# One written order for all steps of a DeltaNet and mixer kernel in place of a planner

## The chip, the cores and the metric

The kernel runs on one core of one Trainium2 chip. The core has five engines with a queue of instructions each: TensorE (PE, matrix products; PEld is its weight load), VectorE (DVE), ScalarE (ACT), GpSimd (POOL) and SyncE (SP, which here only issues transfers). Every engine works through its queue strictly in order and waits on semaphores for the others. The metric is the device time of one execution in microseconds (us), as the median of several runs.

## The reference

The inputs are q, k and v of shape (4, 8, 768, 48), beta of (4, 8, 768), U (768 x 32), V (32 x 768), w_ch1 (384 x 1536) and w_ch2 (1536 x 384); the first four are fp32, the weights 64-bit. The first half is a linear attention with the delta rule, token by token for each of the 32 heads:

```python
k_n = k / (norm(k, axis=-1) + 1e-6)
state = zeros((B, H, D, D))
for t in range(S):
    y[:, :, t] = q[:, :, t] @ state              # per head
    v_old = k_n[:, :, t] @ state
    state += beta[:, :, t] * outer(k_n[:, :, t], v[:, :, t] - v_old)
```

The heads are then put side by side (x has shape 4 x 768 x 384), and the second half mixes tokens through a low rank product and channels through an MLP:

```python
u = x + (x.T @ U @ V).T          # over the tokens of a batch
out = u + relu(u @ w_ch1) @ w_ch2
```

## The kernel before, in words

**Tiling.** The 768 tokens of a batch are cut into 12 chunks of 64 tokens, and 6 chunks make a unit; there are 8 units, two to a batch. Within a chunk the token loop is replaced by matrix products and the inverse of a triangular matrix; between chunks runs a recurrence over the state. The MLP works on three groups of 256 tokens a batch.

**A unit.** `load` (its transfers at L531) brings k, q, v and a second copy of k into one of two slots, in pieces of 72 KB through the queues of SP and POOL (the first k pieces through ACT's too). `grams` turns k and q on TensorE (L633), copies them out on ACT (L648) and multiplies (`products`, L661); ACT and DVE take the diagonal blocks (L671, L674) and DVE masks the products with q (L692). `load_beta` (L551 to L577) brings beta over the region of X, turns it on TensorE and spreads it. `norms` works out 1/|k|^2 times beta and scales v (L610). `blocks` inverts the 32-wide diagonal blocks by substitution on DVE (L737 lays them out, L746 and L752 are the 32 steps, L759 returns them) and joins them to the inverses of 64-wide blocks on TensorE (L802, L816, L842 to L863). The units of batch 0 join 16-wide blocks first (L802 and L816).

**The recurrence.** `recur(b)` has for each of the 12 chunks: the product of the state with the k (L1051) on TensorE, its subtraction on DVE that gives z (L1064; in later batches the chain at L1010 to L1043), the state update's product (L1079), its addition on DVE (L1089), and the outputs (L925, L939), which ACT copies into X (L909). When the last chunk of a unit is out, the slot is free and the loads of the unit after next may start.

**Weights.** `load_weights` brings 14 slices of U, V, w_ch1 and w_ch2 as 64-bit numbers of two 32-bit words each into staging regions (the second half of X, `wide`, and hs), issued by SP (L1166; the first by POOL). DVE makes one fp32 word of each pair (L1193, L1199, L1205), with a copy by ACT between that writes the upper 16 bits (L1174), and forms sums of weights at L1119. A slice may be fetched when the slice before it in the same region has been unpacked.

**The MLP.** `front` forms u (L1372 to L1418). `wide` is the first product with 6 channel steps per group. Each step exists in two forms: plain, six matmuls of 128x128 by 256 columns, three to each half (L1475), or parted in four 64x64 quadrants (L410, `crossed`) with a small ACT copy between (L419, `swap`), which avoids a change of TensorE's tiling when it stands next to other quadrant work. ACT applies the relu (L1440), DVE forms sums (L1502, L1509) for a product scheme with 7 products in place of 8, and `narrow` is the second product (L1590) with DVE collecting (L1515) and SP storing (L1521, L1524).

**What sets the order.** Every function above is a generator that yields one step at a time: its engine, a cost, a form of TensorE, the PSUM bank that it takes and those that it gives back, or a list of keys that it needs first. `run` (L343 to L398) is a planner that works while the program is built. At each turn it works out when every waiting step could start (`start_of`, L315), with a clock per engine, costs that are written at the steps, a model of TensorE's clock (`pace`, L293: a factor of 1.9 for slow), of instruction fetches (`late`, L307) and of landings (`landing`, L125); among the steps that could start soonest it takes the one with the lowest place. The places are a table of some 250 entries (`PLACES`, L145), and entries ending in "quad" allow the parted form for a channel step (`form`, L332). All five queues come out of this one order.

```python
def op(engine, cost, mode=None, take=None, give=(), lat=None, ...)      # L103
begin(start(i), 22)                                                     # a part with its place
x = yield op("pe", 0.8, "F", take="pair", words=12, flow=0.64)          # a step of grams
yield need(("wide", i))                                                 # what must be written first
```

A key is emitted when the step that makes it has been written down; a list of needs so holds back the writing of a step. On the chip the program's semaphores hold what the data demand.

Of the kernel before, what the change touches and what calls it, by code (L numbers as in the profile page):

```python
# [1 line left out]

# [5 lines left out]

# [8 lines left out]

# [6 lines left out]

QUADS = ((0, 0), (1, 1), (1, 0), (0, 1))


@with_exitstack
def kernel(
    ctx: ExitStack,  # L30
    tc: tile.TileContext,
    q: bass.AP,
    k: bass.AP,
    v: bass.AP,
    beta: bass.AP,
    moe_U: bass.AP,
    moe_V: bass.AP,
    moe_w_ch1: bass.AP,
    moe_w_ch2: bass.AP,
    out: bass.AP,  # L40
):

    nc = tc.nc  # L50

# [16 lines left out]
    W2 = 2 + 2 * KT  # L68

    const = ctx.enter_context(tc.tile_pool(name="const", bufs=1))  # L70
    single = ctx.enter_context(tc.tile_pool(name="single", bufs=1))
    small = ctx.enter_context(tc.tile_pool(name="small", bufs=2))
    conv = ctx.enter_context(tc.tile_pool(name="conv", bufs=2))
    mix = ctx.enter_context(tc.tile_pool(name="mix", bufs=2))
    scratch = ctx.enter_context(
        tc.tile_pool(name="scratch", bufs=2, space=bass.MemoryType.DRAM)
    )
    psum = ctx.enter_context(
        tc.tile_pool(name="psum", bufs=1, space=bass.MemoryType.PSUM)
    )  # L80

    P = psum.tile([128, 8, 512], FP32, name="P")
    BANK = dict(pair=[0, 2, 4, 6], mix=[6, 7])

    clock = dict(port=0.0, pe=0.8, dve=0.8, act=0.8, pool=0.8, sp=0.8)
    state = dict(now=0.0, mode=None, hw=0.0, slow=1.9, lot=69, fetched=0.0, flow=0.0, span=0)
    free = dict(pair={x: 0.0 for x in range(4)}, mix={})
    done, parts, waits, ready, last = {}, {}, {}, {}, {}  # L90
    asked, missing, awaited, woken, quads = {}, {}, {}, [], set()
    LAT = dict(pe=0.22, dve=0.06, act=0.06, pool=0.1, sp=0.0)
    SWITCH, HOLD, STAY = 0.18, 0.18, 0.15
    LOT, FETCH = 256, 4.1
    SPAN, PHASE = 3.413, 2.0

    def dve(n):
        return (n + 151) / 1000.0

    def act(n):  # L100
        return 0.16 + n / 1200.0

    def op(  # L103
        engine, cost, mode=None, take=None, give=(), lat=None, rush=None, words=0, port=None, flow=None,
        after=(),
    ):
        return dict(
            after=after,
            flow=cost * 0.95 if flow is None else flow,
            e=engine, cost=cost, mode=mode, take=take, give=give, words=words + 0.4,  # L110
            port=engine == "pool" if port is None else port,
            rush=bool(give) if rush is None else rush, lat=LAT[engine] if lat is None else lat,
        )
# [4 lines left out]
    def emitted(key, after=0.0):  # L118
        done[key] = state["now"] + after
# [5 lines left out]
    def landing(packets, each=0.0205):  # L125
        state["hw"] = max(state["hw"], state["now"] + 1.0) + packets * each / 16
        return state["hw"] + 0.4 - state["now"]

    def advance(i, value, at):
        try:  # L130
            s, ready[i] = parts[i].send(value), at
        except StopIteration:
            waits.pop(i, None)
            return
        if isinstance(s, list):
            waits.pop(i, None)
            asked[i], missing[i] = s, {key for key in s if key not in done}
            for key in missing[i]:
                awaited.setdefault(key, []).append(i)
            if not missing[i]:  # L140
                woken.append(i)
        else:
            waits[i] = s

    PLACES = """  # L145
    add_up b0 i0 17.5; add_up b0 i1 115.48; add_up b0 i2 71; add_up b1 i1 10.76; add_up b1 i2 15.15
    add_up b2 i0 54.56; add_up b2 i1 63.94; add_up b2 i2 115.5; add_up b3 i0 -4.22; add_up b3 i1 62.29
    add_up b3 i2 42; blocks n1 40.91; blocks n2 26.26; blocks n3 92.86; blocks n4 49.5; blocks n5 78.95
    blocks n6 36.67; blocks n7 136.31; both -6; channels b0 i0 e1 24.46; channels b0 i0 e2 52.34
    channels b0 i0 e3 47.17; channels b0 i0 e4 51.28; channels b0 i0 e5 -8.66; channels b0 i1 e0 52.04  # L150
    channels b0 i1 e0 quad 1; channels b0 i1 e1 79.42; channels b0 i1 e2 120.05; channels b0 i1 e3 96.5
    channels b0 i1 e3 quad 1; channels b0 i1 e4 13.79; channels b0 i1 e5 26.76; channels b0 i2 e0 quad 1
    channels b0 i2 e1 88.32; channels b0 i2 e1 quad 1; channels b0 i2 e2 92.17; channels b0 i2 e2 quad 1
    channels b0 i2 e3 128.97; channels b0 i2 e4 12; channels b0 i2 e4 quad 1; channels b0 i2 e5 88
    channels b0 i2 e5 quad 1; channels b1 i0 e0 40.95; channels b1 i0 e0 quad 1; channels b1 i0 e1 59
    channels b1 i0 e1 quad 1; channels b1 i0 e2 96.8; channels b1 i0 e2 quad 1; channels b1 i0 e4 91
    channels b1 i0 e4 quad 1; channels b1 i0 e5 69.5; channels b1 i0 e5 quad 1; channels b1 i1 e1 123.7
    channels b1 i1 e1 quad 1; channels b1 i1 e2 47.06; channels b1 i1 e2 quad 1; channels b1 i1 e3 -2.83
    channels b1 i1 e4 -16.29; channels b1 i1 e4 quad 1; channels b1 i1 e5 99.12; channels b1 i1 e5 quad 1
    channels b1 i2 e0 62.73; channels b1 i2 e0 quad 1; channels b1 i2 e2 35.08; channels b1 i2 e3 93.63  # L160
    channels b1 i2 e3 quad 1; channels b1 i2 e4 -29.18; channels b1 i2 e5 10.16; channels b1 i2 e5 quad 1
    channels b2 i0 e0 107; channels b2 i0 e1 41.61; channels b2 i0 e2 12.5; channels b2 i0 e2 quad 1
    channels b2 i0 e3 100.05; channels b2 i0 e3 quad 1; channels b2 i0 e4 17.5; channels b2 i0 e5 68.5
    channels b2 i1 e0 -1.5; channels b2 i1 e0 quad 1; channels b2 i1 e1 107.29; channels b2 i1 e1 quad 1
    channels b2 i1 e2 -7.68; channels b2 i1 e2 quad 1; channels b2 i1 e3 -3.95; channels b2 i1 e4 33.5
    channels b2 i1 e4 quad 1; channels b2 i2 e0 0.4; channels b2 i2 e0 quad 1; channels b2 i2 e1 22.31
    channels b2 i2 e1 quad 1; channels b2 i2 e2 21.63; channels b2 i2 e2 quad 1; channels b2 i2 e3 7.38
    channels b2 i2 e3 quad 1; channels b2 i2 e4 90.57; channels b2 i2 e5 quad 1; copies 0; cut 9
    diagonals n0 h0 -0.5; diagonals n0 h1 107.22; diagonals n1 h0 48.5; diagonals n1 h1 -9.5; diagonals n2 h0 12
    diagonals n2 h1 67.42; diagonals n4 h0 15; diagonals n4 h1 22.77; diagonals n5 h0 66.26; diagonals n5 h1 66.6  # L170
    diagonals n6 h0 49.61; diagonals n6 h1 75; diagonals n7 h0 65.5; diagonals n7 h1 71.44; first 71.59
    first_of_last 8.76; front b0 i0 46.95; front b0 i0 quad 1; front b0 i1 41.01; front b0 i2 58.06
    front b1 i0 30.2; front b1 i1 45.12; front b1 i2 142.26; front b1 i2 quad 1; front b2 i0 46.76
    front b2 i0 quad 1; front b2 i1 6.48; front b2 i1 quad 1; front b2 i2 66.34; front b3 i0 56.8
    front b3 i1 110.5; front b3 i2 18.13; gather b0 i0 h0 c1 70.62; gather b0 i0 h1 c0 116.5
    gather b0 i0 h1 c1 103.04; gather b0 i1 h0 c0 57.42; gather b0 i1 h0 c1 47.56; gather b0 i1 h1 c0 101.5
    gather b0 i1 h1 c1 114; gather b0 i2 h0 c0 78.4; gather b0 i2 h1 c0 54.71; gather b0 i2 h1 c1 59.36
    gather b1 i0 h0 c0 60.5; gather b1 i0 h0 c1 110; gather b1 i0 h1 c1 16.38; gather b1 i1 h0 c0 7
    gather b1 i1 h0 c1 0.46; gather b1 i2 h0 c0 81; gather b1 i2 h0 c1 76; gather b1 i2 h1 c0 93.52
    gather b1 i2 h1 c1 -12; gather b2 i0 h0 c0 67; gather b2 i0 h0 c1 29.97; gather b2 i0 h1 c0 26.5  # L180
    gather b2 i0 h1 c1 46.69; gather b2 i1 h0 c0 12.5; gather b2 i1 h0 c1 4; gather b2 i1 h1 c1 -0.93
# [76 lines left out]
    wide b0 i2 113.63; wide b1 i0 110.97; wide b1 i1 12; wide b1 i2 100.81; wide b2 i1 94; wide b2 i2 81.54  # L258
    wide b3 i1 10; wide b3 i2 -7.5
    """  # L260
    PLACES = dict(x.strip().rsplit(" ", 1) for x in PLACES.replace("\n", ";").split(";") if x.strip())

    def name_of(part):

# [42 lines left out]
    def late(s, at):  # L307

        over = state["lot"] + s["words"] - LOT
        if s["e"] != "pe" or over <= 0:  # L310
            return 0.0, 0.0
# [1357 lines left out]
```

## Time and profile before

The kernel took 611.29 us, the median of 3 runs (608.94 to 613.19).

| | |
|---|---|
| span of the profiled execution | 609.6 us, 24,754 instructions |
| median of the runs | 611.29 us |
| TensorE busy | 569.9 us, 93% |
| VectorE busy | 395.1 us, 65% |
| ScalarE, GpSimd busy | 235.9 us, 97.7 us |
| transfers | 33.34 MB, mean 55 GB/s |
| costliest line | L1590, the second product |

The profile describes one execution, and its times are counted from the span's start. "P<-ut,w_sb" names what an instruction writes and what it reads. In a timeline a row gives the start, the length, the engine and the line, and in brackets how long the engine stood idle before it and what ended that. A matmul on fp32 operands shows as two records, so 210 matmuls are 420 records. VectorE's queue is strictly in order: where one instruction waits, everything behind it waits.

### The profile page before, as it was taken

Reading aid. Unit: us, or ns where it says so; the run is one execution under the profiler, and the core shown is the slowest. Engines: PE = TensorE matmul, PEld = TensorE weight load, DVE = VectorE, ACT = ScalarE, POOL = GpSimd, SP = SyncE. Lnnn points to the kernel's source line nnn. Section 1 sums busy time; section 2 is a strip of 40 time slices with the busy share of each in tenths; the row PEclk is TensorE's granted clock in tenths of the full one; section 3 lists DMA queues with packets and bytes.
Section 4 is the critical chain, followed back from the end, with each engine's and each line's share of the span. In section 5 each row is a group of like instructions: output and inputs, shape, how many; then the busy total and the mean of one; then the engine's idle time right before and its main releaser. Section 6 shows DMA issues by size and latency. Waiting matters only on the chain.

```text
span 609.6 us, 24754 instructions
## 1 busy us (share of the span) xinstructions
PE 569.9 (93%) x11178; PEld 480.4 (79%) x11178; DVE 395.1 (65%) x972; ACT 235.9 (39%) x498; POOL 97.7 (16%) x169
## 2 busy tenths in 40 slices
PE   4797776999999998999999899999999999999997
PEld 4697765788889787888879767988888768656997
DVE  5889966798893232899899428998993225332542
ACT  3566863634242343344332633244225321344000
POOL 8321124420010126003005230020001000000000
PEclk9656575899999999999999999999999999999999
DMA  9951759610000156101006133020000000000000
GB/s 142 165 149 52 252 173 166 120 41 4 28 3 6 44 81 117 49 2 41 29 3 100 49 74 49 16 53 3 30 2 3 30 3 1 26 1 1 19 34 26
DMA packets 63849, 33.34 MB, mean 55 GB/s; under 512 B 50816, under 2 KB 61824, under 8 KB 63744
## 3 DMA queue, kind: packets, MB, share of 16 engines
q1 hardware_dynamic: 56800, 23.21, 17.7%
q0 software_dynamic: 5344, 8.27, 6.5%
q8 instruction: 87, 1.43, 1.0%
q10 hardware_dynamic: 1600, 0.30, 0.3%
q14 instruction: 18, 0.15, 0.1%
HBM read 27.03 MB, written 4.72 MB: 52 GB/s over the span
## 4 chain that ended last, share of the span: by engine, by line
PE 71%; DVE 8%; ACT 2%; issue 2%; DVEq 0%; ACTq 0%
PE P L1590 22%; PE P L1475 13%; PE P L410 12%; PE P L1275 7%; PE P L633 2%; PE P L661 2%; DVE xt L752 2%; DVE prod L746 2%; PE P L1034 2%; PE P L1010 1%; PE P L925 1%; PE P L1079 1%; ACT hs L1440 1%; PE P L1372 1%; PE P L939 1%
## 5 line engine op out<-in xcount | busy, mean ns | idle before, releaser
L1475 PE MATMUL P<-ut,w_sb 128*128 128x256 f32 x420 | 97.2, 384 | 0.2
L1475 PEld LDWEIGHTS P<-ut,w_sb 128*128 128x128 f32 x420 | 77.8, 190 | 11.2 <-ACT hs L1440 0.9
L1590 PE MATMUL P<-w_sb,hs 128*128 128x192 f32 x456 | 79.5, 329 | 0.0
L1590 PEld LDWEIGHTS P<-w_sb,hs 128*128 128x128 f32 x456 | 74.0, 190 | 2.8 <-ACT hs L1440 0.9
L1515 DVE TENSOR_TENSOR X<-X,P 128x192 f32<-128x192 f32 x85 | 29.6, 352 | 62.7 <-PE P L1590 55.1
L752 DVE TENSOR_TENSOR xt<-xt,prod 128x112 f32<-128x112 f32 (+21 forms) x200 | 64.6, 323 | 6.9
L746 DVE TENSOR_TENSOR prod<-gs,xt 128x112 f32<-128x112 f32 (+21 forms) x200 | 64.1, 321 | 4.9
L410 PE MATMUL P<-ut,w_sb 64*64 64x256 f32 x912 | 62.5, 384 | 1.2 <-ACT hs L1440 0.2
L1440 ACT ACTIVATE hs<-P 128x512 f32<-128x512 f32 x54 | 32.3, 597 | 74.0 <-PE P L1475 56.1
L531 POOL DMA_DIRECT2D slot<-in_k_dram x44 | 28.9, 664 | 95.4 <-PE P L1079 94.5
L1590 PE MATMUL P<-w_sb,S 128*128 128x192 f32 x240 | 41.6, 328 | 0.0
L633 PE MATMUL P<-ident,slot 128*128 128x128 f32 x192 | 31.6, 317 | 8.6 <-DMA slot<-in_k_dram 7.0
L909 ACT COPY X<-P 64x192 f32<-64x192 f32 x96 | 30.0, 312 | 24.0 <-PE P L939 22.0
L1590 PEld LDWEIGHTS P<-w_sb,S 128*128 128x128 f32 x240 | 39.0, 190 | 0.2
L410 PEld LDWEIGHTS P<-ut,w_sb 64*64 64x64 f32 x912 | 29.7, 133 | 10.5 <-ACT hs L1440 1.7
L648 ACT COPY slot<-P 128x768 f32<-128x768 f32 x30 | 23.5, 801 | 36.1 <-PE P L633 35.9
L1089 DVE TENSOR_TENSOR s<-s,P 128x192 f32<-128x192 f32 x40 | 14.0, 351 | 33.0 <-PE P L1079 30.2
L633 PEld LDWEIGHTS P<-ident,slot 128*128 128x128 f32 x192 | 25.8, 163 | 11.7 <-issue 9.7
L1275 PE MATMUL P<-slot,w_sb 128*128 128x384 f32 x96 | 34.6, 492 | 0.1
L881 ACT COPY slot<-zz 32x384 f32<-32x384 f32 x64 | 32.3, 509 | 6.1 <-DVE zz L759 4.7
L661 PEld LDWEIGHTS P<-slot 48*64 48x64 f32 x1536 | 29.3, 150 | 6.5 <-issue 2.8
L661 PE MATMUL P<-slot 48*64 48x64 f32 x1536 | 31.9, 237 | 0.6 <-ACT slot L648 0.5
(157 smaller groups left out, 966.1 us busy)
## 6 DMA issues: line engine op xcount, KB each, us to landing
out_dram<-X SPq DMA_DIRECT2D x22, 192.0 KB, 1.9
X<-in_moe_w_ch_dram SPq DMA_DIRECT2D x10, 384.0 KB, 4.2
wide<-in_moe_w_ch_dram SPq DMA_DIRECT2D x10, 384.0 KB, 4.5
slot<-in_k_dram SPq DMA_DIRECT2D x48, 72.0 KB, 5.0
slot<-in_k_dram POOLq DMA_DIRECT2D x44, 72.0 KB, 5.1
slot<-in_q_dram POOLq DMA_DIRECT2D x32, 72.0 KB, 5.0
slot<-in_q_dram SPq DMA_DIRECT2D x32, 72.0 KB, 5.0
slot<-in_v_dram POOLq DMA_DIRECT2D x32, 72.0 KB, 3.0
```

The lines of the kernel that those rows point to most:

```text
L410: nc.tensor.matmul(to[half(g)], w[half(r), half(g)], x[half(r)], start=start, stop=stop, skip_group_check=True,)
L633: nc.tensor.transpose(p_t[:, c // 3, c % 3], t[:, c, 2 * j : 2 * j + 2].rearrange("p s d -> p (s d)"), ident,)
L661: nc.tensor.matmul(p_g[half(g ^ (par * i)), par, c], kq[rows, c, j, 0, half(g)], kq[rows, c, j, i, half(g)], start=True, stop=True,)
L746: nc.vector.tensor_tensor(out=prod, in0=gb[:, :, j : j + 1, j + 1 :].to_broadcast([128, split, m, w]), in1=xb[:, :, 0:m, j : j + 1].to_bro ...
L752: nc.vector.tensor_tensor(out=xb[:, :, 0:m, j + 1 :], in0=xb[:, :, 0:m, j + 1 :], in1=prod, op=ALU.subtract,)
L881: nc.scalar.copy(pg[quarter(i), :, at, :, a : a + BK], cut(zc, h)[quarter(i)].rearrange("p r (c j) t -> p r c j t", j=2),)
L909: nc.scalar.copy(x[half(c % 2), c // 2, 4 * D * g : 4 * D * (g + 1)].rearrange("p (j r d) -> p r j d", r=2, d=D), states(p_y)[half(g)],)
L1275: nc.tensor.matmul(to, w, t, start=start, stop=stop, skip_group_check=True)
L1440: nc.scalar.activation(hs[:, fs[0] : fs[1] + 1 : fs[1] - fs[0]], p_f, ACTF.Relu)
L1475: nc.tensor.matmul(p_f[:, x], w(x, t), ut[:, t], start=(t == 0), stop=(t == KT - 1))
L1515: nc.vector.tensor_tensor(out=to, in0=to, in1=p, op=ALU.add)
L1590: nc.tensor.matmul(to, of[0], of[1], start=of[2], stop=of[3], skip_group_check=True)
```

## The change

The planner goes, with its clocks, models, costs and places. In its place stands `ORDER`, a text of 2,228 tokens. Each token is the number of a part (in the order in which parts are begun); it writes down that part's next step. Where the step takes a PSUM bank, the token names it (14.0), and a "q" picks the parted form of a channel step. `op` keeps only the engine, the form and the bank. All five queues change their order over the whole program.

```diff
-    def op(engine, cost, mode=None, take=None, give=(), lat=None, rush=None, words=0, port=None, flow=None, after=()):
-        return dict(after=after, flow=..., e=engine, cost=cost, mode=mode, take=take, give=give, ...)
+    ORDER = """
+    1 0 1 0 1 0 1 0 22 1 38 22 38 22 21 22 14.0 21 2 21 37 151 21 20 151 15.1 36 2 36 167 26 166.2 36 167 26
...
+    """
+    def op(engine, mode=None, take=None):
+        return dict(engine=engine, mode=mode, take=take)
...
     def run():
-        ...                       # choose the soonest step with the lowest place
+        wake()
+        for token in ORDER.split():
+            i, bank, quad = (token.partition('q')[0] + '.').split('.')[0], token.partition('.')[2], 'q' in token
+            step = waits[int(i)]
+            if isinstance(step, tuple):
+                step = step[quad]
+            mode[0] = step['mode'] or mode[0]
...
+            advance(int(i), int(bank) if bank else first)
+            wake()
```

Four needs are written out that the planner's timing had met by itself:

```diff
         def outputs(c, s_old):          # the last chunk of a unit frees the slot
+            if cu == UC - 1:
+                yield [('y', b, c - 1), ('y', b, c - 2)]
                 emitted(('rec', n))
         def put(c, y, p_y):             # X also stages beta and weights
-            yield need(("stored", b - 2, c // 2)) if b > 1 else []
+            yield ([('stored', b - 2, c // 2)] if b > 1 else [('beta', 1)] if b == 0 else [('weights', W2 + HF - 1)])
     def wide(b, i):                     # the last batch
-        yield need(("front", b, i), ("half" if b == LAST else "narrow", *before(b, i), *[3] * (b == LAST)))
+        yield need(('front', b, i), *([('half', *before(b, i), 3), ('summed', *before(b, i), 6)] if b == LAST else [('narrow', *before(b, i))]))
         def relu(fs, ms, p_f):          # hs also stages weights
+            yield [('weights', 7)]
```

The sixth channel step of a group is left with the plain form alone:

```diff
-            yield (op("pe", 1.3, "F", take=("mix", y % 2), words=12), op("pe", 0.87, "Q", take=("mix", (0, 1)), words=32))
-            if parted():
+            plain = op('pe', mode='F', take=('mix', y % 2))
+            last = y == len(PAIRS) - 1
+            yield (plain if last else (plain, op('pe', mode='Q', take=('mix', (0, 1)))))
+            if parted() and (not last):
```

As built, both programs hold the same instructions apart from three channel steps that take the plain form instead of the parted one (18 matmuls at L1475 more, 72 at L410 fewer, 3 copies at L419 fewer). Around the recurrence of batch 0 the new order places the chunks between the joins of unit 1 (L802 and L816), and the last weight slice behind the tenth of the chunks counted from 0; at the start it puts one mask (L692) ahead of the first `norms`, both turns of q ahead of the second step of `load_beta` on TensorE, and one k load ahead of the second beta load on POOL.

More of the change, by code (lines that the diff above doesn't have):

```diff
@@ L82 @@
-    P = psum.tile([128, 8, 512], FP32, name="P")
-    BANK = dict(pair=[0, 2, 4, 6], mix=[6, 7])
[L87 to L113, printed above, removed]
+    const = ctx.enter_context(tc.tile_pool(name='const', bufs=1))
@@ L123, in emitted, with advance @@
                 woken.append(i)
[L125 to L129, printed above, removed]
+    def advance(i, value):
+        waits.pop(i, None)
         try:
-            s, ready[i] = parts[i].send(value), at
+            step = parts[i].send(value)
         except StopIteration:
-            waits.pop(i, None)
             return
-        if isinstance(s, list):
-            waits.pop(i, None)
-            asked[i], missing[i] = s, {key for key in s if key not in done}
+        if isinstance(step, list):
+            missing[i] = {key for key in step if key not in done}
             for key in missing[i]:
@@ L142, in advance @@
         else:
[L143 to L150, printed above, removed]
@@ L307, in late @@
[L307 to L311, printed above, removed]
-        crossed = at + cost_of(s) * (1 - over / s["words"])
-        return crossed, max(0.0, state["fetched"] - crossed)
-    def start_of(i, s):
-        e, was = s["e"], last.get(i)
-        at = max(was[1] if was and was[0] == e else ready[i], clock[e])
-        if s["port"]:
-            at = max(at, clock["port"])
-        if any(x not in done for x in s["after"]):
-            return None
-        at = max([at] + [done[x] for x in s["after"]])
-        if s["take"]:
-            when = opens(s)
-            if when is None:
-                return None
-            at = max(at, when[0])
-        if s["mode"] and s["mode"] != state["mode"]:
-            at += SWITCH
-        return at, late(s, at)[1]
@@ new lines, in advance, with begin, wake @@
+            waits[i] = step
+    def begin(part):
+        parts.append(part)
+        advance(len(parts) - 1, None)
+    def wake():
+        while woken:
+            advance(woken.pop(0), None)
+    def run():
+        wake()
[5 more added lines that the diff above has]
+            mode[0] = step['mode'] or mode[0]
+            fixed = step['take'][1] if isinstance(step['take'], tuple) else None
+            first = fixed[0] if isinstance(fixed, tuple) else fixed
+            advance(int(i), int(bank) if bank else first)
+            wake()
+        assert not waits and not awaited
@@ L1030, in recur @@
[L1030 to L1032 removed]
+                        nc.tensor.matmul(states(p_b)[half(g), par, j], kq[half(par, D), cu, j, 0, half(g)], states(s_old)[half(par, D), g, j], start=True, stop=True)
+                    emitted(('b', b, c))
+                    if cu < UC - 1:
+                        begin(outputs(c, s_old))
@@ L1209, in load_weights @@
-            emitted(("freed", i))
-            emitted(("weights", i), 0.1)
+            if slices[i][2] == 'f':
+                top, rest, low = (t.rearrange('p (a d) -> p a d', a=2) for t in (top, rest, low))
+            begin(upper_half(i, halves(i, dst, FP16)[1], top))
+            yield op('dve')
+            nc.vector.tensor_scalar(out=rests[:, 0:n], in0=h, scalar1=3, scalar2=65535, op0=ALU.logical_shift_left, op1=ALU.bitwise_and)
+            yield need(('upper half', i))
+            yield op('dve')
```

1460 lines of the change are left out of this document (504 added, 956 removed), and 57 rows, old and new, of the table ORDER.

## The prediction

> **What bounds the kernel now.** I read the page's busy shares and clock line first, then the busy time by stretches, then the chain that ended last, then VectorE's own timeline where that chain leaves TensorE.
>
> ```profile
> PE 569.9 (93%) x11178; PEld 480.4 (79%) x11178; DVE 395.1 (65%) x972; ACT 235.9 (39%) x498; POOL 97.7 (16%) x169
> ...
> PEclk9656575899999999999999999999999999999999
> ```
>
> ```profile
> 15.24:30.48 15.24, 11.61 (x246) 10.26 (x246) 13.47 (x45) 8.59 (x18) 5.47 (x8) 0.61 1.04 165
> 30.48:45.72 15.24, 15.24 (x356) 14.59 (x356) 13.45 (x31) 9.57 (x20) 3.45 (x6) 0.50 0.52 149
> 45.72:60.96 15.24, 11.94 (x452) 10.72 (x450) 14.07 (x42) 9.21 (x18) 1.80 (x3) 0.67 0.17 52
> 60.96:76.20 15.24, 11.93 (x392) 11.22 (x396) 13.80 (x24) 12.64 (x24) 1.65 (x4) 0.55 0.78 252
> 76.20:91.44 15.24, 11.77 (x472) 10.66 (x473) 10.29 (x21) 10.33 (x20) 3.86 (x6) 0.72 0.55 173
> 91.44:106.68 15.24, 10.33 (x321) 8.92 (x316) 9.93 (x20) 5.65 (x13) 6.11 (x10) 0.50 0.96 166
> ```
>
> ```profile
> 107.00:606.40 499.40, 489.33 (x8826) 1.00 0.16 33
> ```
>
> The stretch rows give length, busy time of PE, PEld, DVE, ACT and POOL, the granted clock and the DMA share; the last row has PE alone. There are two kernels here. From 107 us to the last matmul PE is busy 489.33 of 499.40 us at clock 1.00: a reordering can win at most the 10.1 us of gaps. Before it, PE runs at 0.50 to 0.72 and stands idle about a quarter of the time; DVE is over 88% busy from 15 to 76 us and then a third idle (20.22 busy of the last 30.48 us). So the prefix is a chain of DVE work until 76 us, and after that a chain that waits.
>
> ```profile
> 55.93 0.35 DVE L1064 TENSOR_TENSOR z<-slot,P 128x192 f32<-128x192 f32 x1 [0.17 <-PE P L1051]
> ...
> 70.49 0.36 DVE L1064 TENSOR_TENSOR z<-slot,P 128x192 f32<-128x192 f32 x1 [0.26 <-PE P L1051]
> ...
> 84.37 0.56 DVE L1193 TENSOR_SCALAR power<-X 128x768 int32<-128x768 int32 x1 [1.05 <-DMA X<-in_moe_w_ch_dram]
> ...
> 86.36 0.34 DVE L1064 TENSOR_TENSOR z<-slot,P 128x192 f32<-128x192 f32 x1
> ...
> 87.41 0.56 DVE L1193 TENSOR_SCALAR power<-wide 128x768 int32<-128x768 int32 x1 [0.71 <-DMA wide<-in_moe_w_ch_dram]
> ...
> 94.17 0.56 DVE L1193 TENSOR_SCALAR power<-X 128x768 int32<-128x768 int32 x1 [1.87 <-DMA X<-in_moe_w_ch_dram]
> ...
> 99.72 0.56 DVE L1193 TENSOR_SCALAR power<-wide 128x768 int32<-128x768 int32 x1 [1.59 <-DMA wide<-in_moe_w_ch_dram]
> ...
> 105.89 0.35 DVE L1064 TENSOR_TENSOR z<-slot,P 128x192 f32<-128x192 f32 x1
> ```
>
> L1064 is one step of batch 0's recurrence over 12 chunks; the rows shown are chunks 1, 2, 5 and 11. L1193 opens the unpacking of a weight slice. DVE works strictly in its written order, so each L1193 that waits for its slice holds up every chunk behind it: 1.05 + 0.71 + 1.87 + 1.59 = 5.2 us in four waits. When chunk 11 is done, PE goes on with batch 1 and the MLP and does not stop again.
>
> **Part 1: three channel steps in the plain form.** As built, the parted form at L410 falls from 456 to 384 matmuls and the plain one at L1475 rises from 210 to 228; two records each. That is 19 to 16 and 35 to 38 steps.
>
> ```profile
> L1475 PE MATMUL P<-ut,w_sb 128*128 128x256 f32 x420 | 97.2, 384 | 0.2
> L410 PE MATMUL P<-ut,w_sb 64*64 64x256 f32 x912 | 62.5, 384 | 1.2 <-ACT hs L1440 0.2
> ```
>
> A plain step costs 97.2 / 35 = 2.78 us, a parted one 62.5 / 19 = 3.29: three make -1.5 us, all of it on PE, which is the bound there. Against that PE changes its form 134 times instead of 131. No row isolates a change; the planner's own constant is 0.18 us, so +0.5 (between 0 and +1.0). Part: **-1.0**. Three ACT copies of the parted form ("seen") go too, off the path.
>
> **Part 2: the early order.** One mask is put ahead of the first norms, the second beta step behind both q turns on PE, one k load ahead of the second beta load on POOL, and SP's and POOL's loads are interleaved one by one. Counting DVE's instructions in both orders, each with its mean of before, the first substitution ends with 3.1 us more work ahead of it and the second with 0.4 more. DVE is 88 to 92% busy from 15 to 61 us in the rows above, so I take the later figure, **+0.4**, in the landing below (ends -1 and +3.1).
>
> **Part 3: recurrence against joins and weights.** Chunk 2 follows chunk 1 by 14.6 us (55.93 to 70.49), because unit 1's joins stand between on PE:
>
> ```profile
> 59.19 1.54 PE L802 MATMUL P<-zz,hs 64*64 64x16 f32 x48
> ...
> 63.72 5.31 PE L816 MATMUL P<-zz,S 64*64 64x16 f32 x96 [1.11 <-ACT S L778]
> ```
>
> The new order puts chunks between these joins. Counted the same way, chunk 2 has 7.9 us less DVE work ahead of it and chunk 5 5.6 us less, but the weight slices keep their places in DVE's work within 0.7 us until the very last one. So chunk 5 comes about 4 us sooner, and the chain is then set by the slices:
>
> ```profile
> 79.57 1.20 SPq L1166 DMA_DIRECT2D X<-in_moe_w_ch_dram  x2
> 81.69 1.20 SPq L1166 DMA_DIRECT2D wide<-in_moe_w_ch_dram  x2
> 86.49 2.05 SPq L1166 DMA_DIRECT2D X<-in_moe_w_ch_dram  x2
> ...
> 90.52 1.20 SPq L1166 DMA_DIRECT2D wide<-in_moe_w_ch_dram  x2
> ```
>
> ```profile
> 85.44 1.03 DVE L1205 SCALAR_TENSOR_TENSOR w_sb<-X 128x768 uint16<-128x768 uint32 x1
> ```
>
> ```profile
> 87.46 4.14 POOL L531 DMA_DIRECT2D slot<-in_k_dram  x6 [13.25 <-PE P L1079]
> 91.59 2.62 POOL L531 DMA_DIRECT2D slot<-in_q_dram  x4
> ```
>
> Call the four slices A, B, C, D. They land 4.8, 5.7, 7.7 and 9.2 us after issue (84.37, 87.41, 94.17, 99.72). C reuses A's buffer and is issued when L1205 of A ends (85.44 + 1.03); D reuses B's. C and D are slow where A and B are not because batch 1's k and q loads start at 87.46, when chunk 5's state update has freed the slot. With chunk 5 sooner these ten loads go ahead of C. They hold 720 KB; at the 252 GB/s moved in the 60.96 to 76.20 row, that is 2.9 us.
>
> [...]
>
> D then lands at 99.7 + 0.4 (part 2) - 1.0 (D is issued 3.1 us after B landed; counted as in part 2, 2.1 us of work stand there now) + 2.9 = 102.0. In the new order only D's L1193 (0.56 us) stands between its landing and chunk 11: D's L1199 and L1205 and a sum at L1119 move behind it.
>
> ```profile
> L1205 DVE SCALAR_TENSOR_TENSOR w_sb<-wide,X 128x768 uint16<-128x768 uint32 x5 | 5.1, 1024 | 0.0
> ...
> L1199 DVE TENSOR_SCALAR X<-wide 128x768 int32<-128x768 int32 x5 | 2.8, 553 | 0.0
> ...
> L1119 DVE TENSOR_TENSOR w_sb<-w_sb 128x576 f32<-128x576 f32 x5 | 3.7, 752 | 0.0
> ```
>
> ```profile
> 111.54 1.44 DVE L674 SCALAR_TENSOR_TENSOR slot<-P,even,slot 128x192 f32<-128x192 f32 x4 [2.38 <-ACT slot L671]
> ```
>
> Chunk 11 starts at 102.6 instead of 105.89: **-3.3**. What is moved is 1.02 + 0.55 + 0.75 = 2.3 us, and it falls into the 2.38 us that DVE waits ahead of L674; were that cover gone, up to 2.3 would come back. Ends of this part: nothing gained if A is issued 3.3 us later; about -10 if no slice is waited for (the 5.2 us of waits, the 2.3 moved, and half of the other 5.1 us that DVE is idle after 76 us).
>
> **Part 4: the long part.** The chain after 107 us shows two bare ACT copies of the turned k and q:
>
> ```profile
> 114.47 0.81 ACT slot L648
> ...
> 118.48 0.81 ACT slot L648
> ```
>
> ```profile
> PE P L860 <- issue: 1.5, 1, 1.5
> ```
>
> The new order sets MLP channel steps between the products there (the first channel step comes at PE's 1,358th matmul and not the 1,418th), so both are covered: -1.6. Of the other 8.5 us of gaps I take a tenth, -0.9; the longest one, 1.5 us, waits for nothing that the trace shows, and I leave it. Part: **-2.5**, between +10 (the rival below) and -8.
>
> **Part 5: the four waits made explicit** hold a step back from being written down; the built program has fewer semaphore waits on PE (102 against 114), 3 fewer on DVE, 2 more on ACT and 2 fewer on POOL. With a fixed order nothing queues behind them that was not already behind: 0.
>
> **Sum.** -1.0 - 3.3 - 2.5 = -6.8 us on the execution's span of 609.6: 602.8. The median of the runs, 611.29, lies 1.7 above that span, so 604.5.
>
> **Rivals.** *The interleaving pays in full*: the loads do not delay C and D, and chunks 6 to 11 run without a stall. For it: DVE has only 75.0 us of work in the 91.4 us of the six rows. Against: a landing of at least 4.8 us with 2.1 us of unpacking behind it give one slice per buffer about every 7 us. Chunk 11 at 96 to 100, in all -9.4 to -13.4 us: 598 to 602, down to 592 with all gaps of part 4.
>
> *No change to speak of*: the early 3.1 us are not caught up, A is issued at 82 to 84, and C and D land as late as the slack won. For it: from 46 to 76 us DVE has under 3 us of idle to give. Then part 3 gives 0 and part 4 half: 609.6 - 2.3 + 1.7 = 609, 607 to 615.
>
> *Slower: PE reaches its producers too early.*
>
> ```profile
> L1440 ACT ACTIVATE hs<-P 128x512 f32<-128x512 f32 x54 | 32.3, 597 | 74.0 <-PE P L1475 56.1
> ...
> L1475 PEld LDWEIGHTS P<-ut,w_sb 128*128 128x128 f32 x420 | 77.8, 190 | 11.2 <-ACT hs L1440 0.9
> ```
>
> The old planner took whatever was ready by its clock; a written order packed by a model has less slack, and each consumer of a relu (L1440) that stands one step too early stalls PE by part of its 0.6 us, with nothing else written that could run. In before such waits total 0.9 us at L1475. At 0.25 us for each of 54 it is +13.5; with parts 1 and 3, 609.6 + 9.2 + 1.7 = 620.5. It decides from a mean wait of about 0.2 us a relu.
>
> *The clock.* The rows at 45.72 and 76.20 show 0.67 and 0.72, which at a clock of either 0.5 or 1 means 5.2 and 6.7 us at full speed. If chunks between the joins thin PE out and half of these 11.9 us are granted 0.5, it is +3.0 on the sum: 607.5. [...]
>
> **Chances.** The forecast (601 to 607) 0.36, full pay 0.15, no change 0.23, the clock 0.05, slower 0.21. About 1% is what a measurement of this kernel can tell from no change, so faster means under 605.2 and slower over 617.4. Faster: 0.15 and two thirds to three quarters of 0.36, 0.41. Slower: 0.21. The rest, 0.38, is within 1%. The range leaves out the far half of full pay's tail and the upper half of slower: 594 to 620.5.
>
> **What would show it.** Right: chunk 2 near 63 us, chunk 5 near 82, POOL's k loads at 83, a DVE wait for D that ends near 102, chunk 11 right behind it, no bare L648 in the chain after 107, L1475 x456. Wrong: a first L531 of batch 1 ahead of A's issue, DVE waits moved to the masks or to beta, PE gaps after 107 us above 12 us, or a clock line that rises later than slice 8.

## The result and the profile after

The changed kernel takes 609.41 us, the median of 20 runs (606.46 to 612.87), against 611.89 for the kernel before in 20 runs beside it: 0.9963 of before, 95% interval 0.9947 to 0.9979. It is faster by 0.4%, where 1.1% was forecast. In a second set of runs (f1 below) it was 0.9991 (0.9963 to 1.0019), so the gain is between nothing and a half per cent.

The profiled execution is the slowest of its 20 (its span is 611.2 us, its own time 612.87, 3.5 us over the median), and that of f1 the slowest of its 12, which has to be kept in mind with every comparison below. The page of the changed kernel, its busy shares and clock line:

```profile
PE 570.2 (93%) x11070; PEld 485.8 (79%) x11070; DVE 388.7 (64%) x972; ACT 232.1 (38%) x495; POOL 97.8 (16%) x169
...
PEclk9955665799999999999999999999999999999999
```

The same stretches as in the prediction (length, busy time of PE, PEld, DVE, ACT and POOL, granted clock, DMA share, GB/s), for the changed kernel:

```profile
15.24:30.48 15.24, 11.66 (x211) 10.38 (x210) 10.93 (x38) 8.77 (x20) 5.45 (x8) 0.99 1.06 156
30.48:45.72 15.24, 13.66 (x302) 13.14 (x304) 14.40 (x33) 7.54 (x15) 2.23 (x3) 0.50 0.34 89
45.72:60.96 15.24, 13.36 (x480) 12.42 (x478) 14.35 (x44) 10.12 (x20) 2.90 (x6) 0.50 0.37 117
60.96:76.20 15.24, 14.19 (x437) 13.65 (x438) 13.16 (x25) 10.58 (x20) 0.82 (x2) 0.61 0.62 199
76.20:91.44 15.24, 11.27 (x432) 10.18 (x432) 8.37 (x16) 11.02 (x22) 8.26 (x12) 0.60 0.57 155
91.44:106.68 15.24, 8.02 (x269) 7.27 (x272) 8.17 (x18) 5.99 (x11) 0.00 (x0) 0.51 0.81 172
```

The 0.99 of the first row is no faster clock: six matmuls that last 0.85 us in before at a granted clock of 1.00 (13.27 us) and 1.51 us at 0.50 (14.94 us) last 1.54 us at 18.24 us here. By these lengths the clock was the half one for a part of that row at least, and the row can't be compared with the 0.61 of before.

DVE is now idle for almost half of the time from 76 to 107 us (16.5 busy of 30.5, before 20.2), and PE is idle more too. VectorE's timeline says why (start, length, engine, line; in brackets the idle time before and what ended it; L680 is the chunk step that was L1064 and L694 the state's addition that was L1089; L777, L783 and L786 are the steps of unpacking):

```profile
64.13 0.35 DVE L680 TENSOR_TENSOR z<-slot,P 128x192 f32<-128x192 f32 x1 [0.72 <-PE P L673]
...
81.04 0.36 DVE L694 TENSOR_TENSOR s<-s,P 128x192 f32<-128x192 f32 x1 [0.83 <-issue]
82.63 0.35 DVE L680 TENSOR_TENSOR z<-slot,P 128x192 f32<-128x192 f32 x1 [1.23 <-PE P L673]
82.90 1.02 DVE L786 SCALAR_TENSOR_TENSOR w_sb<-X 128x768 uint16<-128x768 uint32 x1
...
90.99 0.56 DVE L777 TENSOR_SCALAR power<-X 128x768 int32<-128x768 int32 x1 [3.95 <-DMA X<-in_moe_w_ch_dram]
...
98.67 0.56 DVE L777 TENSOR_SCALAR power<-wide 128x768 int32<-128x768 int32 x1 [5.19 <-DMA wide<-in_moe_w_ch_dram]
...
110.56 0.36 DVE L680 TENSOR_TENSOR z<-slot,P 128x192 f32<-128x192 f32 x1
```

Chunk 2 comes at 64.13 and not 70.49, chunk 5 at 82.63 and not 86.36, as forecast. But chunk 11 comes at 110.56, 4.7 us later than before, and in between stand two waits for slices, 3.95 and 5.19 us, 9.1 where the four of before made 5.2. SP's queue and GpSimd's for the same time:

```profile
83.94 1.98 SPq L757 DMA_DIRECT2D X<-in_moe_w_ch_dram  x2
87.07 1.20 SPq L757 DMA_DIRECT2D wide<-in_moe_w_ch_dram  x2
...
93.27 1.22 SPq L757 DMA_DIRECT2D X<-in_moe_w_ch_dram  x2
...
102.46 1.58 SPq L757 DMA_DIRECT2D wide<-in_moe_w_ch_dram  x2
```

```profile
85.25 2.92 POOL L301 DMA_DIRECT2D slot<-in_k_dram  x4 [4.39 <-PE P L690]
88.17 2.62 POOL L301 DMA_DIRECT2D slot<-in_q_dram  x4
```

These are the slices A, B, C and D. A is issued at 83.94 (before 79.57) and lands 7.0 us later (before 4.8); B is issued at 87.07 and takes 11.6 us (before 5.7). GpSimd's eight loads for batch 1 start at 85.25, between the two. In the chain that ended last, B's transfer is the longest piece between 76 and 112 us, 30% of that time:

```profile
87.70 10.84 DMA wide<-in_moe_w_ch_dram
```

Behind chunk 11 it is the other way round. PE alone from the end of chunk 11 to the last matmul, before and then after:

```profile
106.23:606.40 500.17, 490.04 (x8842) 1.00 0.16 33
```

```profile
110.91:608.00 497.09, 486.30 (x8735) 1.00 0.16 34
```

In these two profiles that part is 3.1 us shorter. PE does 3.7 us less there, and its gaps (the time in which it stands idle) grew from 10.1 to 10.8 us.

### The profile page after: what moved, and what is told of

Same layout as the page of the kernel before. It is cut to its first block, busy times and chain, and to the rows that moved or that the text cites. A ratio compares the mean times of both kernels' runs of the same rounds, so it can differ in the third digit from the quotient of the medians.

```text
span 611.2 us, 24520 instructions
## 1 busy us (share of the span) xinstructions
PE 570.2 (93%) x11070; PEld 485.8 (79%) x11070; DVE 388.7 (64%) x972; ACT 232.1 (38%) x495; POOL 97.8 (16%) x169
## 4 chain that ended last, share of the span: by engine, by line
PE 63%; DVE 27%; issue 4%; ACT 3%; DMA 3%; ACTq 0%; DVEq 0%; SPq 0%
PE P L1102 21%; PE P L1014 10%; PE P L201 8%; PE P L838 7%; DVE xt L460 6%; DVE prod L459 6%; PE P L398 3%; PE P L375 2%; DMA wide<-in_moe_w_ch_dram 2%; PE P L604 1%; DVE gs L450 1%; PE P L649 1%; PE P L597 1%; DVE slot L417 1%; PE P L690 1%
## 5 line engine op out<-in xcount | busy, mean ns | idle before, releaser
L1014 PE MATMUL P<-ut,w_sb 128*128 128x256 f32 x456 | 106.3, 385 | 0.8 <-ACT hs L984 0.6
L1014 PEld LDWEIGHTS P<-ut,w_sb 128*128 128x128 f32 x456 | 84.1, 190 | 14.4 <-issue 1.8
L201 PE MATMUL P<-ut,w_sb 64*64 64x256 f32 x768 | 52.3, 385 | 1.6 <-ACT hs L984 1.3
L694 DVE TENSOR_TENSOR s<-s,P 128x192 f32<-128x192 f32 x40 | 13.9, 349 | 37.9 <-PE P L690 35.4
L398 PE MATMUL P<-slot 48*64 48x64 f32 x1536 | 33.7, 246 | 4.5 <-ACT slot L386 4.5
L398 PEld LDWEIGHTS P<-slot 48*64 48x64 f32 x1536 | 30.8, 158 | 8.6 <-ACT slot L386 6.0
L567 POOL MEMSET slot<- 32x384 f32 x32 | 13.3, 422 | 124.1 <-PE P L538 70.2
L838 PE MATMUL P<-slot,w_sb 128*128 128x384 f32 x96 | 33.1, 486 | 0.0
L201 PEld LDWEIGHTS P<-ut,w_sb 64*64 64x64 f32 x768 | 25.1, 133 | 8.9 <-ACT hs L984 2.3
```

Of the source, the lines that this page charges most:

```text
L201: nc.tensor.matmul(to[half(g)], w[half(r), half(g)], x[half(r)], start=start, stop=stop, skip_group_check=True)
L398: nc.tensor.matmul(p_g[half(g ^ par * i), par, c], kq[rows, c, j, 0, half(g)], kq[rows, c, j, i, half(g)], start=True, stop=True)
L838: nc.tensor.matmul(to, w, t, start=start, stop=stop, skip_group_check=True)
L1014: nc.tensor.matmul(p_f[:, x], w(x, t), ut[:, t], start=t == 0, stop=t == KT - 1)
```

## The experiments

In the diffs "prefix" means all steps up to chunk 11 of batch 0 and its output, some 480 of 2,228, and "rest" what follows; the steps are the same and only their order is taken from one kernel or the other. Ratios are to the kernel before on the same chip.

### The written order alone, and the three plain steps

```diff
 ORDER = """      # h1: every step where the planner of before put it, channel steps as before
-    channels (b0 i2), (b1 i1), (b1 i2), sixth step: parted
+    channels (b0 i2), (b1 i1), (b1 i2), sixth step: plain          # e1 and h2
```

In e1 and h2 a few steps beside two of the three change places too.

Expected of e1:

> The order of before written out as tokens, all steps as before but for the three channel steps, which take the plain form; the four needs are in. Theory (the three forms are worth -1.0, the written order and the needs nothing): 611.9 - 1.0 = 610.9. Rival (the forms are all of the gain): 609.4. Rival (writing the order out changes what the chip does): off 611.9 by more than 3.

Expected of h1:

> The order of before, every instruction of every engine as in the kernel before, only produced from tokens. If writing the order out changes nothing: 1.000 of before, within 0.003. If the written-out program differs by itself: 1.004, as e1_forms_only, and then the forms cost nothing.

Expected of h2:

> As h1 with the three channel steps in the plain form. If the forms cost what e1_forms_only showed: 1.004 and h1 at 1.000. If they are worth the -1.0 us of the forecast: 0.998. If e1_forms_only was chance: 1.000 to 1.001 by its 0.8 us of TensorE busy time.

Measured: e1 1.0041 (1.0015 to 1.0067), h1 1.0011 (0.9984 to 1.0038), h2 1.0030 (1.0011 to 1.0050). Writing the order out costs nothing that these runs can tell. The three plain steps alone make the kernel slower than before by 0.3 to 0.4%, about 2 us (h2 beside h1 by 1.2 us, which is within the noise), where -1.0 was forecast. PE alone behind chunk 11, in e1 (the row of before is above):

```profile
108.61:609.00 500.39, 490.84 (x8734) 1.00 0.16 33
```

The steps themselves did get cheaper, from 97.2 + 62.5 = 159.7 us in the prediction's rows to 106.4 + 52.7 = 159.1 in e1's:

```profile
L1016 PE MATMUL P<-ut,w_sb 128*128 128x256 f32 x456 | 106.4, 385 | 0.2
L203 PE MATMUL P<-ut,w_sb 64*64 64x256 f32 x768 | 52.7, 384 | 1.1 <-ACT hs L986 0.2
```

All of PE's work together became 0.8 us longer (1.7 in h2 beside h1, 491.40 against 489.74). In this order the plain steps stand among parted work, and behind its first 1,200 matmuls PE changes its tiling 113 times where it was 105. With the 1.5 us that the prediction's prices give for the steps, that is 8 changes for 0.8 + 1.5 = 2.3 us, 0.29 each (0.40 by h2 and h1), if the changes are what costs; g3's expectation below takes 1.35 us for the steps, which no row shows, and so 0.27. The 0.8 is not all of the 2 us; where the rest of it arises is not shown.

### Prefix and rest exchanged

```diff
 ORDER = """
-    prefix: after    rest: after
+    prefix: before   rest: after         # e2
+    prefix: after    rest: before        # e3, the three steps plain
+    before up to the first state (55 us), after from there             # e4
```

Expected of e2:

> The order of before up to chunk 11 of batch 0, the order of after from there. Theory (the long part gained 3.1, 609.6 - 105.9 = 503.7 against 611.2 - 110.6 = 500.6, and the new prefix gives some of it back): 611.9 - 3.1 = 608.8, chunk 11 near 106, faster than after. Rival (the gain lies in the prefix and the profiled execution is not typical): 611, slower than after.

Expected of e3:

> The order of after up to chunk 11 of batch 0, the order of before from there, with the three plain channel steps. Theory (new prefix 0.6 to 4.7 later, forms -1.0): 611.5 to 615.6, chunk 11 at 106.5 to 110.6. Rival (the gain lies in the prefix): 609.4 or less, chunk 11 at 104.

Expected of e4:

> The order of before only up to the first state of the recurrence (55 us), the order of after from there. Theory (the early order of after costs 1.6 us at the end of the second substitution, 57.77 against 56.20, and the later slices are late for that reason): 609.4 - 1.6 = 607.8, or better where slice A is issued ahead of the loads of batch 1. Rival (the slices are late whatever the early order is, since the loads of batch 1 start with chunk 5): 609.4, landings of A and B still 7 and 11.6 us after their issue.

Measured: e2 0.9971 (0.9949 to 0.9993), e3 1.0089 (1.0055 to 1.0124), e4 0.9977 (0.9954 to 0.9999). The rest of after is worth about 3 us or more under either prefix (e2 against e1; after against e3). The prefix of after is worth nothing under either: with the rest of before it costs 0.5% (e3 against e1), with that of after it and the prefix of before are the same (0.9963 and 0.9991 against 0.9971). So the gain that was measured is made behind chunk 11: e2, with nothing but the new rest, has all of it. Chunk 11 ended at 106.9 in e2, at 108.2 in e3 and at 111.1 in e4. e4 says that the early order is not at fault: with that of before the slices are late all the same. e3 had a wide spread (613.7 to 621.8) with a profile near its lower end, and why its median is as high as 616.6 is not explained.

### What makes the slices late

f1 is the changed kernel again. f2 lets all k and q loads of unit 2 go through SP, at their written places (the second copy of k stays where it was); f3 does that to e2, and g1 to the kernel before (in its h1 form). f4 changes the order around slice A alone, and g2 is f2 and f4 together.

```diff
         for g in halves:                                                   # f2, f3, g1, g2
-            if g and (n, name) != (0, 'k'):
+            if g and (n, name) != (0, 'k') and not (n == NU and name in ('k', 'q')):
                 e = 'pool'
```

```diff
 ORDER = """                                                              # f4, g2
+    upper_half of the slice before A             (ACT)
     three copies of diagonals of unit 1          (ACT)
-    upper_half of the slice before A             (ACT)
...
+    its last unpacking step (DVE), issue of A (SP)
     chunk 3's state, chunk 4                     (DVE)
-    its last unpacking step (DVE), issue of A (SP)
```

Expected of f1:

> The changed kernel once more, on the chip of the next three runs, with a profile of another execution. 609.4 as before. If the profiled execution of 611.2 was late by its prefix (chunk 11 at 110.6), this one has chunk 11 about as much earlier as its span is shorter, and 500 us behind chunk 11.

Expected of f2:

> The changed kernel with the k and q loads of unit 2 all on SP, at their places in the written order, so that they cannot run ahead of the slices C and D; nothing else differs. Theory (the loads that GpSimd issues at 85 us delay A and B, whose landings take 7.0 and 11.6 us and make 9.1 us of VectorE waits): A and B land within 6 us, C and D are issued 4 to 6 us sooner, chunk 11 is 4 to 6 us sooner; 604 to 606, unless TensorE then waits for the last k. Rival (the slices are late by themselves, transfers are slow at that time for another reason): 609.4 and landings as before. Rival (slower: the last k is issued behind D and lands after chunk 11): 612 or more with a TensorE wait for in_k at the turn after chunk 11.

Expected of f3:

> The order of before up to chunk 11, that of after from there (as e2_before_prefix, 0.9971 of before), with the same loads on SP. Theory: C and D, 7.7 and 9.2 us after their issue in the profile of before, land in 5 to 6 us; chunk 11 3 to 4 us sooner, 0.991 to 0.993 of before. Rival (hidden anyway): as e2_before_prefix, 0.997.

Expected of f4:

> The changed kernel with one slice unpacked sooner: ScalarE's copy of it ahead of three diagonal copies, its last VectorE step and the issue of slice A ahead of chunk 3's state; only the order differs. Theory (A is late because the chunks that were moved forward stand ahead of the unpacking): A issued at 81 instead of 83.9, landed before the loads of batch 1 begin to move, chunk 6 about 4 us sooner, chunk 11 2 to 3 us sooner, B still late; 606.5 to 608. Rival (the loads that start at 85 us set the landing of B whatever A does): chunk 11 unchanged, 609.4.

Expected of g1:

> The kernel before, every engine's order as it was, with the k and q loads of unit 2 all on SP at their places in its written order. Theory (the loads that GpSimd issues at 87 us hold up C and D in this kernel too): C and D land in 5 to 6 us and not in 7.7 and 9.2, chunk 11 at 103 to 104 and not 106: 0.995 to 0.997 of before. Rival (hidden behind VectorE's other waits): 1.000.

Expected of g2:

> The changed kernel with both edits, the loads of unit 2 on SP (alone 0.9951 of before) and slice A unpacked and issued sooner (alone 0.9957). Theory (both work on the one chain of slices, each takes a part of the wait): A issued at 80, B at 84, chunk 11 at 102 to 103: 0.990 to 0.993. Rival (the two take the same wait): 0.995, chunk 11 at 104.

Expected of h3:

> The order of before up to chunk 11, that of after from there, loads of unit 2 on SP, as f3_before_prefix_loads_on_sp: 0.9923 again, within 0.003. If the six runs of it were lucky: 0.995.

| | ratio to before | 95% interval | end of chunk 11, us |
|---|---|---|---|
| f1 | 0.9991 | 0.9963 to 1.0019 | 112.35 |
| f2 | 0.9951 | 0.9925 to 0.9978 | 104.2 |
| f3 | 0.9923 | 0.9893 to 0.9954 | 104.0 |
| h3, f3 again | 0.9918 | 0.9894 to 0.9943 | 105.1 |
| f4 | 0.9957 | 0.9932 to 0.9982 | 107.4 |
| g1 | 0.9942 | 0.9920 to 0.9964 | 105.1 |
| g2 | 0.9952 | 0.9920 to 0.9984 | 106.2 |

In f2, SP's queue and VectorE's waits:

```profile
82.48 1.55 SPq L757 DMA_DIRECT2D X<-in_moe_w_ch_dram  x2
85.62 1.20 SPq L757 DMA_DIRECT2D wide<-in_moe_w_ch_dram  x2
```

```profile
87.91 0.56 DVE L777 TENSOR_SCALAR power<-X 128x768 int32<-128x768 int32 x1 [2.31 <-DMA X<-in_moe_w_ch_dram]
...
92.55 0.56 DVE L777 TENSOR_SCALAR power<-wide 128x768 int32<-128x768 int32 x1 [2.17 <-DMA wide<-in_moe_w_ch_dram]
...
103.84 0.35 DVE L680 TENSOR_TENSOR z<-slot,P 128x192 f32<-128x192 f32 x1
```

B lands 6.9 us after its issue (in g2, with the same edit, 5.0), where it took 8.1 to 11.8 us in the five profiles that have the new order and GpSimd's loads at 84 to 88 us (after, f1, e3, e4, g4). A's 5.4 us proves nothing, since A took 5.2 to 8.1 us in those five. Chunk 11 starts at 103.84 and not 110.56 or 112.00. A part of that was there before the edit could act (chunk 5 at 81.16 and not 82.63 or 85.80); from chunk 5 to chunk 11 it is 22.7 us against 27.9 and 26.2. PE waits only 0.2 us for a last k behind it. Its time, 608.5 us, stays above the 604 to 606 of the theory. The eight loads that GpSimd issued beside B were what held it. The same edit gives the kernel before 0.6%, and with the prefix of before and the rest of after it makes the fastest kernel of all, twice: 0.9923 and 0.9918, about 5 us under before, and under the changed kernel. VectorE's waits in it (f3), after which only PE's wait of 1.6 us for a late q is left of the transfers:

```profile
84.88 0.56 DVE L779 TENSOR_SCALAR power<-X 128x768 int32<-128x768 int32 x1 [0.92 <-DMA X<-in_moe_w_ch_dram]
...
88.25 0.56 DVE L779 TENSOR_SCALAR power<-wide 128x768 int32<-128x768 int32 x1 [0.43 <-DMA wide<-in_moe_w_ch_dram]
```

By what mechanism the eight loads hold B up is not shown. B took 8.1 to 11.8 us beside them and 6.9 without them, but in f2 SP issues all eight behind D, from 97.99 us on, when B had landed at 92.55, so that f2 changes the time of the loads together with their queue.

f4 moved A's issue to 80.08 as meant, and the wait went on to B:

```profile
80.08 2.04 SPq L759 DMA_DIRECT2D X<-in_moe_w_ch_dram  x2
86.55 1.20 SPq L759 DMA_DIRECT2D wide<-in_moe_w_ch_dram  x2
```

```profile
94.32 0.56 DVE L779 TENSOR_SCALAR power<-wide 128x768 int32<-128x768 int32 x1 [3.79 <-DMA wide<-in_moe_w_ch_dram]
```

A is no longer waited for (of the others, C still for 1.56 us), and chunk 11 is 3 to 5 us sooner than in the two profiles of the changed kernel. g2 is no faster than either edit alone, against the theory. In its profile VectorE waits only 0.9 us for slices between 76 and 107 us, but 5.7 us for PE's product ahead of z (f2: 1.8): with the slices in time, PE is what the chunks wait for.

### The parted form in the new order

```diff
 ORDER = """      # g4: the changed kernel; g3: f3
-    channels (b0 i2), (b1 i1), (b1 i2), sixth step: plain
+    channels (b0 i2), (b1 i1), (b1 i2), sixth step: parted
```

Expected of g3:

> As f3_before_prefix_loads_on_sp (0.9923 of before), with the three channel steps in the parted form again; TensorE then changes its tiling 103 times behind the first 1200 matmuls and not 110. Theory (a change costs about 0.27 us of busy time: e1_forms_only had 8 more of them and was 0.8 us busier where the steps alone give -1.35): -7 x 0.27 + 1.35 = -0.5: 0.991 to 0.992. Rival (the plain form is the gain it was forecast to be): +1.0, 0.994.

Expected of g4:

> The changed kernel with the three channel steps in the parted form again, nothing else. Theory as for the run before: TensorE's busy time behind chunk 11 0.5 us less than the 486.3 of the changed kernel, the time 0.5 less. Rival (the forecast's own term): 1.0 more.

In these two kernels the parted step takes both banks of the MLP at places where the plain neighbours' sums are still in one of them, so part of the sums of those three groups is changed; the instructions are the kernel's. Measured: g3 0.9966 (0.9948 to 0.9985) against 0.9923 and 0.9918, g4 1.0013 (0.9993 to 1.0033) against 0.9963 and 0.9991. PE behind chunk 11 in g3, and the same in f3:

```profile
105.70:603.20 497.50, 484.93 (x8842) 1.00 0.17 34
```

```profile
103.99:601.50 497.51, 485.57 (x8734) 1.00 0.17 35
```

The busy time falls by 0.64, near the -0.5 of the theory, but the gaps grow by as much, from 11.9 to 12.6, and the stretch is as long as before. The 0.4% that g3 is slower can so not be found in this stretch of the two profiles. As tried here, the plain form is the better one in the new order. Whether the shared banks or the form make the difference is left open.

## Why the prediction was right or wrong

**The time.** Forecast 604.5, measured 609.41: inside the range of 594 to 620.5, but a little over a third of the gain (2.5 of 6.8 us). What came true is the rival called "no change to speak of" (607 to 615, with 609 worked out and a chance of 0.23), in the main by its own mechanism: A issued at 82 to 84 (87.11 in f1), part 3 giving 0 and part 4 giving something. That its 609 is met so closely is luck, since it also has part 1 at -1.0 and the waits at C and D, and the waits came at A and B.

**Part 3 is the step that failed.** Its first half held: chunks 2 and 5 came at 64.13 and 82.63 (forecast near 63 and 82), GpSimd's loads at 85.25 (forecast 83). What failed is "the weight slices keep their places in DVE's work within 0.7 us until the very last one", and that it was taken as if work were time. Counted over the traces in the prediction's way (every VectorE instruction ahead, with its mean of before), the last unpacking step of the slice before A, which frees A's buffer, has 1.5 us more work ahead of it, and so has that of A. And the chunks that were put ahead of it wait: in before a single state addition stands between its second and its last step, now three steps of chunks 4 and 5, with 0.83 and 1.23 us of waiting (the rows at 81.04 and 82.63 above). First before, then after:

```profile
77.49 0.55 DVE L1199 TENSOR_SCALAR X<-X 128x768 int32<-128x768 int32 x1
78.23 0.35 DVE L1089 TENSOR_TENSOR s<-s,P 128x192 f32<-128x192 f32 x1 [0.19 <-PE P L1079]
78.51 1.03 DVE L1205 SCALAR_TENSOR_TENSOR w_sb<-X 128x768 uint16<-128x768 uint32 x1
```

```profile
79.10 0.85 DVE L783 TENSOR_SCALAR X<-X 128x768 int32<-128x768 int32 x1
79.87 0.34 DVE L680 TENSOR_TENSOR z<-slot,P 128x192 f32<-128x192 f32 x1
```

ScalarE's part of the unpacking (L763), which L786 needs, stands behind the diagonals' copies:

```profile
79.15 0.51 ACT L563 COPY slot<-zz 32x384 f32<-32x384 f32 x1
79.68 0.32 ACT L541 COPY zz<-P 128x192 f32<-128x192 f32 x1
80.03 1.03 ACT L563 COPY slot<-zz 32x384 f32<-32x384 f32 x2
81.08 1.05 ACT L763 CAST w_sb<-power 128x768 f16<-128x768 f32 x1
```

So A was issued at 83.94 and not at 79.57; f4, which moves these steps, has it at 80.08. The second term was mis-sized too: the ten loads were put at +2.9 us on C and D, and they fell on A and B instead, with +2.2 and +5.9 (in f1 +0.5 and +4.0). The landing of D was forecast for 102.0; D was issued only at 102.46. In place of -3.3 us at chunk 11 the two profiles show +4.7 and +6.1. With e3 and g4 there are four profiles of the new prefix, with chunk 11 ended at 107.4 to 112.35 us, beside five of the old one (before, e1, e2, h1, h2) at 106.1 to 109.8; the means differ by +2.2. Over many runs the prefix is worth between 0 (e2 beside after) and +0.5% (e3 beside e1).

**Part 4 came near the size by luck and had the wrong reason.** Forecast -2.5; the two profiles show -3.1 (500.17 to 497.09). That is not a measure of the order alone: h1, with the instructions of before, shows 497.75 behind a later chunk 11, and e2, with the new rest and the old prefix, 499.17. Over many runs e2 puts the new rest, plain steps included, at 0.3%, some 2 us. The forecast took its gain from gaps, and they grew: 10.1 us in before and 8.0 in h1, 10.8 in after and 12.4 in e2. PE's own work fell by 3.7. Every kernel with the rest of before shows 489.7 to 491.4 us of it, every one with the rest of after in the plain form 485.5 to 486.9. The saving is spread over many groups, with one place that can be seen at once, the products of the last batch, before and after:

```profile
L1275 PE MATMUL P<-slot,w_sb 128*128 128x384 f32 x96 | 34.6, 492 | 0.1
```

```profile
L838 PE MATMUL P<-slot,w_sb 128*128 128x384 f32 x96 | 33.1, 486 | 0.0
```

What makes the same matmuls shorter in the new order is open: no run takes it apart.

**Part 1** was wrong in sign for the order in which it was worked out: -1.0 forecast, about +2 in e1 and h2. The two groups of steps fell by 0.6 us (159.7 to 159.1) where 1.5 was forecast, and all of PE's work rose. The 8 changes of tiling more in that order were not counted, because the count that was used (134 against 131) was that of the new order; that they are what costs is argued and not shown. The 0.18 us for one change, from which the +0.5 came, is a constant of the planner that no run shows; what the runs give, if the changes are what costs, is 0.29 to 0.40. **Part 2** held: the second substitution ended at 55.8 to 57.8 us in six of the seven profiles with the early order of after (59.5 in f1) and at 56.1 to 57.4 with that of before, and e4 shows nothing won by the old early order. **Part 5** held: h1 is 1.0011.

**The other rivals.** PE did not come too early: its gaps behind chunk 11 are 10.8 us, 1.9 of it for the relu (0.6 at the plain step, 1.3 at the parted one), where the rival needed 13.5. Full pay did not come in the changed kernel. The clock rival came in part: the rows at 45.72 and 76.20 show 0.50 and 0.60 where they were 0.67 and 0.72; what that cost by itself was not measured. Its +3.0 is too small by its own working: by the six matmuls of before that last 0.85 us at 1.00 and 1.51 us at 0.50, 5.95 us of work at the full clock last some 10.6 us at the half one, which is +4.6 as an estimate. And that a thinner PE brings the lower clock is not shown: in the row at 30.48 of before PE is busy for all of the 15.24 us, at 0.50, and in the row at 45.72 it is busy for 13.36 us at 0.50 after the change and for 11.94 at 0.67 before.

## What to carry to other kernels

An order written over all engines binds each queue only by itself: GpSimd's loads stood at chunks 8 to 11 in the text and ran right behind chunk 5, as soon as their slot was free, ahead of slices that another engine needed sooner. Loads that must not overtake belong in the queue of what they must follow; that one line was worth 0.4 to 0.6% in every kernel that it was tried on alone (f2 beside f1, f3 beside e2, g1 beside before), about as much as the whole new order or more. When work is moved ahead of a transfer's issue, sum the waits that come with it and not only its durations.

## What the runs showed that was not expected

The kernel before, e1, h1 and h2 have the same instructions in the same order up to chunk 11, and chunk 11 ended at 106.2, 108.6, 109.8 and 106.1 us in their profiles. A small part of it can be seen early. The same six matmuls in the profile of before and in that of e1:

```profile
13.27 0.85 PE L633 MATMUL P<-ident,slot 128*128 128x128 f32 x6 [1.39 <-DMA slot<-in_q_dram]
```

```profile
13.37 1.51 PE L377 MATMUL P<-ident,slot 128*128 128x128 f32 x6 [1.39 <-DMA slot<-in_k_dram]
```

They waited equally long (the transfer that the trace names as the last differs), and the one took 0.85 us and the other 1.51, the length that six such matmuls have in before at 14.94 us, where the granted clock is 0.50. (The row of e1 for this place shows 1.00, so that the half clock there is read from the length alone.) More of it arises later: D landed 9.2, 10.0, 10.5 and 7.9 us after its issue (in the same order of the four), and that is where h2 gains on e1, with chunk 5 at 87.86 and 87.87. Why D's transfer differs so is not shown. A difference of 2 to 3 us in the prefix between two profiles says nothing by itself here; only medians over many runs do. And chunk 11's time is not passed on in full: h1's came 3.5 us later than that of before, and its last matmul 1.2 us later (607.5 against 606.3).
